# Attention feature sums moved from GpSimd to TensorE strips, with a later second decode and another streamed output weight pair

## The chip, the cores and the metric

One NeuronCore of a Trainium2 chip runs the whole program. The metric is the device time of one execution in microseconds (us), as the median of the runs shown.

## What is computed

A linear attention, and then a gated projection on its output:

```
proj = q @ w_phi;  proj -= max(|proj|) over the features;  phi = [exp(proj), exp(-proj)]   (the same for k)
kv  = sum over s of phi(k)[s, f] * v[s, d]
z   = sum over s of phi(k)[s, f]
att = (phi(q) @ kv) / (phi(q) @ z + 1e-6)
out = ((x @ w_a) * (x @ w_b)) @ w_out          with x = att, heads side by side
```

There are 8 batches of 8 heads, 576 positions, 64 channels a head and 128 features. x is 4608 x 512, w_a and w_b are 512 x 1536, and w_out is 1536 x 512. The three weights come as 64-bit floats and are turned into pairs of 32-bit floats (a high and a low part) on the core.

## The kernel before

The program has two stages, one after the other.

**Attention.** Two heads make a pair, and there are 32 pairs. `attention` (L259) walks i from 0 to 33. Of pair i it does the projections (`project_first`, `project_last`); of pair i-1 the product of features and values (`kv_products`); of pair i-2 the numerator and denominator (`num_products`, `den_products`), whose division (`reciprocals`) follows in steps placed by `turn`, four turns to a pair. TensorE takes its products strictly in the order in which they are written, since `pe` (L64) ties each to the one before. Three double banks of PSUM (`duo`, L263) go round among pq, pk, pn and pd.

The key features of a pair are `e` (128 positions by 2 heads by 4 chunks by 2 signs by 128 features), and `er` holds those of the last 64 positions of two pairs at once. For the queries the maximum runs over partitions, so GpSimd finds it with two all-reduces a pair (L169, tile mb), and VectorE subtracts it (L170). The feature sums z are made by `summed` (L175): GpSimd adds the four chunks to two (L180) and these to one (L182), VectorE adds the rest `er` (L185), and then `z_products` (L197) sums over the partitions by four products with a column block of ones, each for one 32-column strip of the array, into the third part of the PSUM tile kv. `kv_out` copies kv to the tile back, `turned_kv` transposes it (pt) and VectorE copies that to kvh, which the numerator and denominator need.

**Projection.** From L691 on, 12 blocks of 768 tokens follow: 6 with the first half of the hidden features (p = 0) and the same 6 with the second half (p = 1). `moe_block` (L522) uses seven products of half-size matrices in place of eight (`winograd`, L432, three quarters q a block), and each of these from three products of high and low parts. Their weights stand in DRAM (kept) and come back through a ring of four tiles (`refill`, L658): each time a product is done, `feed` (L700) fetches the next. Of w_out, ten pairs of factors stay on chip for all blocks of a half, and the last, a single one (`streamed`, L654), comes through the ring in each block.

**Decoding.** `load_factors` (L318) turns weights into factors: for each of two halves a load (raw, L327), one ScalarE and four VectorE operations, then seven sums and splits with a store each (L353). All of these transfers go through the queue of SyncE (SP). The first half's decoding is spread over the attention by `between` (L675). The second half's begins in block 0, a step at a time from `feed` (L710), at 1.2 steps a product; these steps are not held behind other work (`placed`, L638, holds those of the first half), so the scheduler may draw them forward.

Of the kernel before, what the change touches and what calls it, by code (L numbers as in the profile page):

```python
# [18 lines left out]
P = 128  # L19
# [4 lines left out]
LAG = 2  # L24
# [3 lines left out]
LAST_RATE = 1.2  # L28
# [7 lines left out]
def tile_kernel(ctx, tc, qP, km, kr, vm, vr, w_phi, eye, w_a, w_b, w_out, out):  # L36
# [56 lines left out]
    marks, loads, feeds, st = [], [], [], {}  # L93

    def attention_consts(a1, duo):
# [31 lines left out]
    def features(u, y, n, a1, a2):  # L127
# [3 lines left out]
        d = a1.tile([P, 2, n, F], F32, tag=f"d{n}", name=f"d_{u}")  # L131
# [25 lines left out]
    def project_last(i, a1, a2, consts, duo):  # L157
# [16 lines left out]

    def summed(i, a1, a2):  # L175

        e, er = st["e", i], st["er", i]
        two = a1.tile([P, 2, 2, 2 * F], F32, tag="two", name=f"two_{i}")
        ev = e.rearrange("p j c s f -> p j c (s f)")
        nc.gpsimd.tensor_tensor(two, ev[:, :, 0:2], ev[:, :, 2:4], op=ALU.add)  # L180
        z = st["z", i] = a2.tile([P, 2, 2 * F], F32, tag="z", name=f"z_{i}")
        nc.gpsimd.tensor_tensor(z, two[:, :, 0], two[:, :, 1], op=ALU.add)  # L182
        rows = heads[i % 2]
        rv = er.rearrange("p j c s f -> p j (c s f)")
        nc.vector.tensor_tensor(z[rows], z[rows], rv[rows], op=ALU.add)  # L185
# [11 lines left out]
    def z_products(i, consts):  # L197
        for n, (j, s) in enumerate(itertools.product(range(2), range(2))):
            mm(st["kv", i][strips[n], 2], consts[2], st["z", i][:, j, s * F : (s + 1) * F])

    def kv_out(i, a2):
        back = st["back", i] = a2.tile([P, 3, P], F32, tag="back", bufs=1, name=f"back_{i}")
        nc.scalar.copy(back, st["kv", i])
# [19 lines left out]
    def den_products(i, a2, duo):  # L223
# [7 lines left out]
        dn = a2.tile([P, HALF], F32, tag="dn", bufs=1, name=f"dn_{i}")  # L231
# [27 lines left out]
    def attention(a1, a2, ps, between):  # L259
# [17 lines left out]
        for i in range(NP + LAG):  # L277
# [4 lines left out]
            if num:  # L282
                turned_kv(i - LAG, a2, consts, ps)
            if new:
                project_last(i, a1, a2, consts, duo)
                summed(i, a1, a2)
            if kv_:
                kv_products(i - 1, ps)
            if i + 2 < NP:
                load(i + 2, a1, a2)  # L290
            turn(4 * i + 1)
            if num:
                num_products(i - LAG, a2, duo)
                turn(4 * i + 2)
                den_products(i - LAG, a2, duo)
                steps = reciprocals(i - LAG, a1, a2)
                later.extend((4 * i + 2 + t, steps) for t in REC_TURNS)
            else:
                turn(4 * i + 2)
            if kv_:  # L300
                z_products(i - 1, consts)
                kv_out(i - 1, a2)
            turn(4 * i + 3)
# [5 lines left out]
    outs = [[(p, q, "o", k) for k in FACTORS for q in range(NQ)] for p in range(2)]  # L309
# [8 lines left out]
    def load_factors(p, q, nm):  # L318
# [5 lines left out]
        for i in range(2):  # L324
            f = 2 * (NQ * p + q) + i
            raw = coded.tile([P, DM, 2], U32, tag="raw", name=f"raw_{p}{q}{nm}{i}")
            nc.sync.dma_start(raw.rearrange("p n w -> p (n w)"), src[f * P : (f + 1) * P, :].bitcast(U32))  # L327
# [17 lines left out]
        def stored(*names):  # L345
            for k in names:
# [6 lines left out]
                nc.sync.dma_start(kept[key][:, place], t.bitcast(F32))  # L353
# [78 lines left out]
    def winograd(p, j, q, xs, hs, spaces, feed):  # L432
# [36 lines left out]
        def lo(k, src):  # L469
            nc.vector.tensor_tensor(hs[k][1], src, hs[k][0], op=ALU.subtract)  # L470
# [51 lines left out]
    def moe_block(p, j, xs, x_next, spaces, feed):  # L522
# [75 lines left out]
        product(1, "w12", 1, late_)  # L598
        next(quads[-1])
# [54 lines left out]
    streamed = len(outs[0]) // 2 - 1  # L654
    order = deque(key for p in range(2) for _ in range(NB) for key in [(p, *key) for key in order] + [("o", p, streamed)])
# [17 lines left out]
    early = placed(codes[0])  # L673
# [23 lines left out]
    for p in range(2):  # L697
        own = deque(pair for pair in pairs if pair[:2] == ("o", p) and pair[2] != streamed)

        def feed():  # L700
# [4 lines left out]
            if own:  # L705
# [3 lines left out]
            if p == 0:  # L709
# [54 lines left out]
```

## Time and profile before

| | us |
|---|---|
| Median of 3 runs (lowest to highest) | 1614.45 (1613.93 to 1622.92) |
| The profiled execution, as timed | 1618.62 |
| Its span, from first to last instruction | 1616.8 |
| TensorE busy with products | 1191.3 |
| VectorE busy | 948.6 |
| ScalarE busy | 636.4 |
| GpSimd busy | 258.2 |

The span is that of one execution. Busy time of one engine lies beside that of the others, so these shares do not add up; what counts in a stage is who waits there for whom. The mean granted TensorE clock of the span is 0.862, where 1 stands for 2.4 GHz and the lower of the two levels, 1.2 GHz, would be 0.5. The first projection product begins 752.4 us into the span, so the attention stage takes 752.4 us and the twelve blocks 864.4 us.

### The profile page before, as it was taken

How to read it: one execution, taken by the hardware profiler on the slowest of the kernel's cores; microseconds unless marked ns; L12 is line 12 of the kernel's file. 1: busy time of each engine (PE TensorE's matmuls, PEld its weight loads, DVE VectorE, ACT ScalarE, POOL GpSimd, SP SyncE). 2: the span in 40 equal slices, each digit the busy share in tenths (PEclk: the TensorE clock that was granted, in tenths of full speed). 3: DMA queues.
4: the chain of work that ended last, by engine and by line, in shares of the span. 5: the costliest groups of instructions: out<-in, count | busy, mean ns of one | idle time of the engine just before them, and what ended most of it. 6: DMA issues, size and time to landing. Idle time of an engine off the chain costs nothing.

```text
span 1616.8 us, 20946 instructions
## 1 busy us (share of the span) xinstructions
PE 1191.3 (74%) x7394; PEld 1021.5 (63%) x7394; DVE 948.6 (59%) x1804; ACT 636.4 (39%) x1239; POOL 258.2 (16%) x132
## 2 busy tenths in 40 slices
PE   2736373564536355537798898999999999999998
PEld 2413241332313233325798888999999999999998
DVE  2354353354425346455687886758566686866865
ACT  3324242333324234333354444435344353443532
POOL 2333333334323333341000000000000000000000
PEclk7768687677767677767898999999999999999999
DMA  3225343332323343336988695766789677786774
GB/s 122 80 82 167 113 155 95 94 109 89 114 88 117 106 126 98 112 107 203 377 256 316 226 323 176 241 195 234 238 268 306 186 262 240 233 285 198 258 229 143
DMA packets 135673, 297.67 MB, mean 184 GB/s; under 512 B 22800, under 2 KB 53904, under 8 KB 135568
## 3 DMA queue, kind: packets, MB, share of 16 engines
q1 hardware_dynamic: 135264, 296.20, 55.5%
q8 instruction: 59, 0.97, 0.2%
q14 instruction: 46, 0.38, 0.1%
q10 hardware_dynamic: 304, 0.13, 0.0%
HBM read 234.64 MB, written 61.64 MB: 183 GB/s over the span
## 4 chain that ended last, share of the span: by engine, by line
PE 36%; DMA 10%; DVE 8%; issue 2%; ACT 1%; POOL 0%; SPq 0%; DVEq 0%; ACTq 0%; POOLq 0%
PE pa L430 12%; PE po L430 12%; PE pb L430 12%; DMA back_s<-kept_s 3%; DMA xx<-xnorm 2%; DMA back_w<-kept_w 1%; DVE hl_s L470 1%; DVE top L463 1%; DMA rb<-rec 1%; DMA rec<-r 0%; DVE hl_w L470 0%; DMA xnorm<-x 0%; DMA kept_o<-t_10o_s 0%; DMA raw_11o<-in_w_out 0%; DVE low L510 0%
## 5 line engine op out<-in xcount | busy, mean ns | idle before, releaser
L170 DVE TENSOR_TENSOR p<-p,mb 128x576 f32<-128x576 f32 x64 | 78.5, 1227 | 196.2 <-POOL mb L169 196.2
L78 PE MATMUL kv<-z,ones 128*32 128x128 f32 x256 | 18.6, 373 | 220.8 <-DVE z L185 220.8
L169 POOL PARTITION_ALL_REDUCE mb<-p x64 | 139.4, 2216 | 215.3 <-issue 91.3
L430 PE MATMUL po<-hh_s,back_o 128*128 128x384 f32 x576 | 163.1, 337 | 6.7 <-ACT hh_s L467 6.1
L78 PEld LDWEIGHTS kv<-z,ones 128*32 128x32 f32 x256 | 8.2, 136 | 235.7 <-DVE z L185 231.0
L78 PE MATMUL pn<-eq,kvh 128*64 128x288 f32 x512 | 93.1, 520 | 85.8 <-DVE kvh L211 84.1
L185 DVE TENSOR_TENSOR z<-z,e_r 64x512 f32<-64x512 f32 x32 | 22.0, 686 | 185.1 <-POOL z L182 185.1
L78 PEld LDWEIGHTS pn<-eq,kvh 128*64 128x64 f32 x512 | 47.9, 172 | 124.0 <-issue 93.6
L430 PE MATMUL po<-hh_w,back_o 128*128 128x384 f32 x432 | 119.0, 336 | 2.2 <-ACT o L547 1.6
L430 PEld LDWEIGHTS po<-hh_s,back_o 128*128 128x128 f32 x576 | 105.8, 189 | 9.2 <-ACT hh_s L467 7.4
L180 POOL TENSOR_TENSOR two<-e 128x1024 f32<-128x1024 f32 x32 | 78.2, 2443 | 199.5 <-issue 140.8
L430 PE MATMUL po<-hl_s,back_o 128*128 128x384 f32 x288 | 97.7, 339 | 3.4 <-DVE hl_s L470 3.2
L430 PEld LDWEIGHTS po<-hh_w,back_o 128*128 128x128 f32 x432 | 79.1, 189 | 3.0 <-ACT o L547 1.9
L539 DVE TENSOR_TENSOR o<-po,o 128x384 f32<-128x384 f32 x84 | 46.3, 556 | 56.1 <-PE po L430 42.3
L78 PE MATMUL pq<-q,w 64*128 64x288 f32 x256 | 69.8, 629 | 8.1 <-issue 7.0
L78 PE MATMUL pd<-eq,kvh 128*32 128x288 f32 x512 | 46.5, 490 | 35.9 <-DVE d L134 35.9
L430 PE MATMUL po<-hl_w,back_o 128*128 128x384 f32 x216 | 72.4, 335 | 0.0
L136 ACT ACTIVATE e<-d 128x1024 f32<-128x1024 f32 x32 | 33.8, 1057 | 93.8 <-DVE d L134 93.7
L78 PEld LDWEIGHTS pk<-w,k 64*128 64x128 f32 x512 | 54.1, 292 | 25.0 <-ACT x L221 19.7
L171 ACT ACTIVATE eq<-p 128x1152 f32<-128x1152 f32 x32 | 37.2, 1161 | 80.1 <-DVE p L170 80.1
L78 PE MATMUL kv<-e,v 128*64 128x256 f32 x512 | 67.6, 409 | 1.0 <-ACT e L137 1.0
L78 PE MATMUL pk<-w,k 64*128 64x128 f32 x512 | 55.7, 383 | 13.1 <-ACT x L221 13.1
(320 smaller groups left out, 3349.9 us busy)
## 6 DMA issues: line engine op xcount, KB each, us to landing
back_s<-kept_s SPq DMA_DIRECT2D x144, 512.0 KB
back_w<-kept_w SPq DMA_DIRECT2D x108, 512.0 KB
back_o<-kept_o SPq DMA_DIRECT2D x30, 512.0 KB
q<-in_qP SPq DMA_DIRECT2D x32, 288.0 KB
rb<-rec SPq DMA_DIRECT2D x64, 144.0 KB
xnorm<-x SPq DMA_DIRECT2D x32, 288.0 KB
xx<-xnorm SPq DMA_DIRECT2D x16, 576.0 KB
part<-o SPq DMA_DIRECT2D x48, 192.0 KB
```

The costliest lines, as they stand in the source:

```text
L78: return pe(lambda: nc.tensor.matmul(out, w, x, start=start, stop=stop, skip_group_check=True))
L136: nc.scalar.activation(e[:, :, :, 0], d, AF.Exp)
L169: nc.gpsimd.partition_all_reduce(mb, p32[:, j], P, bass_isa.ReduceOp.absmax)
L170: nc.vector.tensor_tensor(p32[:, j], p32[:, j], mb, op=ALU.subtract)
L171: nc.scalar.activation(eq[:, :, 0], p32, AF.Exp)
L180: nc.gpsimd.tensor_tensor(two, ev[:, :, 0:2], ev[:, :, 2:4], op=ALU.add)
L185: nc.vector.tensor_tensor(z[rows], z[rows], rv[rows], op=ALU.add)
L430: issued[0] = nc.tensor.matmul(*args, skip_group_check=True, **kwargs)
L463: nc.vector.tensor_tensor(to[:, i], acc[k][i], to[:, i], op=ALU.add)
L470: nc.vector.tensor_tensor(hs[k][1], src, hs[k][0], op=ALU.subtract)
L539: nc.vector.tensor_tensor(given[key], x, given[key], op=ALU.add)
```

## The change

1. **Feature sums.** `summed` is gone, and with it the two GpSimd sums and the VectorE sum of each pair. `z_products` now runs over the features themselves: 16 products of `e` (4 chunks by 2 heads by 2 signs) and 4 of `er`, each with a 32-column block of ones into one strip. For `er` the ones are zero in the half of the rows that belongs to the other pair.
2. **Order in the attention.** The products of z follow at once on those of kv, and `turned_kv` now follows in the same pass, between numerator and denominator of the pair before. The steps of the division begin one turn later. Tiles d, back and dn have two buffers.
3. **Second decoding.** Its steps begin in block 1, at 1.45 a product, each held behind the latest marked VectorE operation (also those of `lo` in `winograd` are marked now), and its loads and stores are issued by GpSimd, after the last all-reduce.
4. **w_out.** The streamed entry is now a pair, the two factors w11 and w12 of the last quarter, which is used early in the last part of a block; right after its last use (`spent`) the ring is refilled, where before that came at the block's end. The pairs that stay on chip are fetched at two of three products.

The diff, cut to its core:

```diff
-LAST_RATE = 1.2
+LAST_FROM, LAST_RATE = 1, 1.45
...
-        ones = a1.tile([P, D // 2], F32, name="ones")
+        ones = a1.tile([P, 3, D // 2], F32, name="ones")
         nc.vector.memset(ones, 1.0)
+        nc.vector.memset(ones[D:, 1], 0.0)
+        nc.vector.memset(ones[:D, 2], 0.0)
...
-            nc.gpsimd.partition_all_reduce(mb, p32[:, j], P, bass_isa.ReduceOp.absmax)
+            maxima.append(nc.gpsimd.partition_all_reduce(mb, p32[:, j], P, bass_isa.ReduceOp.absmax))
...
-    def summed(i, a1, a2):
-        e, er = st["e", i], st["er", i]
-        two = a1.tile([P, 2, 2, 2 * F], F32, tag="two", name=f"two_{i}")
-        ev = e.rearrange("p j c s f -> p j c (s f)")
-        nc.gpsimd.tensor_tensor(two, ev[:, :, 0:2], ev[:, :, 2:4], op=ALU.add)
-        z = st["z", i] = a2.tile([P, 2, 2 * F], F32, tag="z", name=f"z_{i}")
-        nc.gpsimd.tensor_tensor(z, two[:, :, 0], two[:, :, 1], op=ALU.add)
...
     def z_products(i, consts):
-        for n, (j, s) in enumerate(itertools.product(range(2), range(2))):
-            mm(st["kv", i][strips[n], 2], consts[2], st["z", i][:, j, s * F : (s + 1) * F])
+        ones, kv = consts[2], st["kv", i]
+        js = list(enumerate(itertools.product(range(2), range(2))))
+        for c in range(NFULL):
+            for n, (j, s) in js:
+                mm(kv[strips[n], 2], ones[:, 0], st["e", i][:, j, c, s], start=(c == 0), stop=False)
+        for n, (j, s) in js:
+            mm(kv[strips[n], 2], ones[:, 1 + i % 2], st["er", i][:, j, 0, s], start=False)
...
             turn(4 * i)
-            if num:
-                turned_kv(i - LAG, a2, consts, ps)
             if new:
                 project_last(i, a1, a2, consts, duo)
-                summed(i, a1, a2)
-            if kv_:
-                kv_products(i - 1, ps)
             if i + 2 < NP:
                 load(i + 2, a1, a2)
             turn(4 * i + 1)
+            if kv_:
+                kv_products(i - 1, ps)
+                z_products(i - 1, consts)
+                kv_out(i - 1, a2)
+            turn(4 * i + 2)
             if num:
                 num_products(i - LAG, a2, duo)
+            if kv_:
+                turned_kv(i - 1, a2, consts, ps)
+            turn(4 * i + 3)
+            if num:
                 den_products(i - LAG, a2, duo)
...
+            queue = nc.gpsimd if p else nc.sync
+            behind(maxima if p else [], lambda: queue.dma_start(raw.rearrange("p n w -> p (n w)"), rows))
...
-                nc.sync.dma_start(kept[key][:, place], t.bitcast(F32))
+                queue.dma_start(kept[key][:, place], t.bitcast(F32))
...
         product(1, "w12", 1, late_)
+        spent()
...
-    streamed = len(outs[0]) // 2 - 1
+    order = deque(key for p in range(2) for _ in range(NB) for key in [(p, *key) for key in order] + [("o", p, 0)])
...
-            if own:
+            if own and used[0] % 3:
...
-            if p == 0:
-                steps(codes[1], 0, LAST_RATE)
+            if p == 0 and j >= LAST_FROM:
+                steps(late, 0, LAST_RATE)
```

On GpSimd the program before alternates between two kinds of work in each pair. These rows of its order are from the third and fourth pair; a bare `ISA` without operands stands at each change of kind, `ISA` with mb is an all-reduce, and two and z are the sums.

```order
L180 TENSOR_TENSOR two_312<-e_279 128x1024
L169 ISA
L169 ISA mb_0_304<-p_2_261 128x576
L169 ISA mb_1_307<-p_2_261 128x576
L182 ISA
L182 TENSOR_TENSOR z_314<-two_312 128x512
L169 ISA
L169 ISA mb_0_419<-p_3_372 128x576
L169 ISA mb_1_422<-p_3_372 128x576
L180 ISA
L180 TENSOR_TENSOR two_427<-e_390 128x1024
```

The same two pairs and the next one on GpSimd in the changed program:

```order
L171 ISA mb_0_312<-p_2_275 128x576
L171 ISA mb_1_315<-p_2_275 128x576
L171 ISA mb_0_438<-p_3_395 128x576
L171 ISA mb_1_441<-p_3_395 128x576
L171 ISA mb_0_584<-p_4_531 128x576
L171 ISA mb_1_587<-p_4_531 128x576
```

The sums are gone and the all-reduces follow on each other. Before, there are 72 bare `ISA` rows on GpSimd; now there are 3, one of them ahead of the first all-reduce.

On TensorE, one pass before, from the sixth pair's projections on (the x behind a row counts products; a product of 32-bit floats takes two instructions):

```order
L78 MATMUL pq_0_632<-q_5_445,w_100 128x288 x2
L78 MATMUL pk_636<-w_100,k_5_443 128x128 x8
L209 MATMUL pt_653<-ident,back_623 128x128 x3
L78 MATMUL pq_1_659<-q_5_445,w_100 128x288 x2
L78 MATMUL kv_677<-e_518,v_4_336 64x256 x8
L78 MATMUL kv_677<-e_r_550,rv_334 64x256 x2
L78 MATMUL pn_701<-eq_418,kvh_657 64x288 x8
L78 MATMUL pd_715<-eq_418,kvh_657 32x288 x8
L78 MATMUL kv_677<-z_564,ones 32x128 x4
```

And one pass of the changed program, of the same pair:

```order
L78 MATMUL pq_0_674<-q_5_448,w_100 128x288 x2
L78 MATMUL pk_678<-w_100,k_5_446 128x128 x8
L78 MATMUL pq_1_700<-q_5_448,w_100 128x288 x2
L78 MATMUL kv_723<-e_549,v_4_328 64x256 x8
L78 MATMUL kv_723<-e_r_580,rv_326 64x256 x2
L78 MATMUL kv_723<-e_549,ones 32x128 x16
L78 MATMUL kv_723<-e_r_580,ones 32x128 x4
L78 MATMUL pn_760<-eq_437,kvh_656 64x288 x8
L204 MATMUL pt_771<-ident,back_754 128x128 x3
L78 MATMUL pd_780<-eq_437,kvh_656 32x288 x8
```

The four products on z have become twenty on e and er, ahead of pn and no longer last in the pass, and pt has gone from the pass's first half to a place between pn and pd.

On SP, the queue before has the second decoding's transfers (raw, and kept from t, of the weights 10a and 10b) among those of the attention's divisions (xnorm, rec, rb):

```order
L327 DMA raw_10b_4473<-in_w_b 128x1024
L353 DMA kept_0_w_4360<-t_10a_w_4357 128x512
L353 DMA kept_0_s_4382<-t_10a_s_4379 128x512
L256 DMA xnorm_79<-x_27_3722 128x576
L353 DMA kept_0_s_4443<-t_10a_s_4440 128x512
L247 DMA rec_72<-r_3880 128x9
L353 DMA kept_0_s_4449<-t_10a_s_4446 128x512
L251 DMA rb_3972<-rec_72 64x576 x2
```

In the changed program these transfers stand on GpSimd, behind the last all-reduce (of pair 31):

```order
L171 ISA mb_1_4244<-p_31_4210 128x576
L323 DMA raw_10a_5197<-in_w_a 128x1024
L323 DMA raw_10a_5252<-in_w_a 128x1024
L349 DMA kept_0_w_5345<-t_10a_w_5342 128x512
L349 DMA kept_0_w_5350<-t_10a_w_5347 128x512
L323 DMA raw_10b_5482<-in_w_b 128x1024
```

All 81 of them, 18 loads and 63 stores, have left SP. Of the second decoding's VectorE rows, 51 stand in the attention before, 25 in block 0, 51 in block 1 and 39 in block 2; now 4 stand in block 0 and 31, 36, 36, 32 and 28 in blocks 1 to 5.

## Rows read from the trace of the kernel before

**Rows 1.** Groups of instructions on GpSimd: count, then busy us, mean ns, idle before.

```profile
L169 POOL PARTITION_ALL_REDUCE mb<-p x64 | 139.4, 2216 | 215.3 <-issue 91.3 <-PE pq L78 18.1 <-PE pk L78 17.5
L180 POOL TENSOR_TENSOR two<-e 128x1024 f32<-128x1024 f32 x32 | 78.2, 2443 | 199.5 <-issue 140.8 <-DVE r L245 15.7 <-DVE w_01b L339 8.0
L182 POOL TENSOR_TENSOR z<-two 128x512 f32<-128x512 f32 x32 | 40.4, 1262 | 66.6 <-issue 57.6 <-ACT t_00a_w L87 7.2
```

**Rows 2.** Timeline of GpSimd: start us, us, instruction, idle before it.

```profile
343.80 2.33 POOL L180 TENSOR_TENSOR two<-e 128x1024 f32<-128x1024 f32 x1 [8.40 <-issue]
...
353.37 4.30 POOL L169 PARTITION_ALL_REDUCE mb<-p  x2 [5.91 <-issue]
364.90 2.33 POOL L180 TENSOR_TENSOR two<-e 128x1024 f32<-128x1024 f32 x1 [7.23 <-issue]
373.14 4.30 POOL L169 PARTITION_ALL_REDUCE mb<-p  x2 [5.91 <-issue]
```

**Rows 3.** Timeline of ScalarE, the inputs of the two at 343.80 and 353.37.

```profile
340.12 0.62 ACT L163 COPY p<-pq 128x576 f32<-128x576 f32 x1
...
341.60 1.04 ACT L137 ACTIVATE e<-d 128x1024 f32<-128x1024 f32 x1
```

**Rows 4.** Stretches: us, busy (instructions) of PE, PEld, DVE, ACT, POOL; clock, DMA.

```profile
0.00:752.00 752.00, 379.08 (x2858) 223.82 (x2858) 336.61 (x548) 270.34 (x434) 258.16 (x132) 0.73 0.35 111
...
387.00:398.00 11.00, 10.85 (x87) 6.73 (x91) 6.42 (x13) 4.41 (x6) 4.72 (x3) 0.74 0.38 122
398.00:407.00 9.00, 8.97 (x95) 5.51 (x87) 5.97 (x6) 6.33 (x9) 3.20 (x2) 1.00 0.44 142
```

**Rows 5.** Timeline of TensorE, two passes in a row.

```profile
387.15 0.65 PE L78 MATMUL kv<-z,ones 128*32 128x128 f32 x8 [23.30 <-DVE z L185]
...
398.05 0.40 PE L78 MATMUL kv<-z,ones 128*32 128x128 f32 x8
...
405.83 1.18 PE L78 MATMUL pd<-eq,kvh 128*32 128x288 f32 x16
```

**Rows 6.** Timeline of the SP queue (transfers issued), one pass.

```profile
396.60 0.38 SPq L247 DMA_DIRECT2D rec<-r  x1
400.05 1.11 SPq L251 DMA_DIRECT2D rb<-rec  x2
401.26 0.52 SPq L234 DMA_DIRECT2D den<-dn  x1
403.41 0.32 SPq L242 DMA_DIRECT2D r<-den  x1
...
406.25 0.38 SPq L121 DMA_DIRECT2D rv<-in_vr  x1
```

**Rows 7.** Timeline of VectorE, behind an all-reduce.

```profile
399.09 1.88 DVE L170 TENSOR_TENSOR p<-p,mb 128x576 f32<-128x576 f32 x1 [2.05 <-POOL mb L169]
```

**Rows 8.** Timeline of TensorE, the attention's opening and end.

```profile
14.68 0.60 PE L78 MATMUL kv<-e_r,rv 128*64 128x256 f32 x4
...
752.41 0.45 PE L430 MATMUL pa<-xw11h,back_w 128*128 128x384 f32 x1 [0.81 <-ACT dn L232]
```

**Rows 9.** Stretches as in rows 4: blocks 0, 1, 2 and 3.

```profile
752.00:821.00 69.00, 55.59 (x292) 53.79 (x293) 47.49 (x103) 28.45 (x67) 0.00 (x0) 0.93 0.89 327
821.00:905.00 84.00, 73.46 (x382) 71.09 (x380) 67.03 (x147) 39.56 (x91) 0.00 (x0) 0.92 0.82 277
905.00:988.00 83.00, 73.19 (x384) 70.77 (x385) 66.19 (x145) 38.99 (x91) 0.00 (x0) 0.94 0.78 266
988.00:1055.00 67.00, 65.36 (x376) 64.89 (x376) 44.85 (x91) 29.31 (x63) 0.00 (x0) 1.00 0.67 218
```

**Rows 10.** Waits of TensorE, 850 to 1010: us in total, times, longest.

```profile
PE pa L430 <- DMA back_s<-kept_s: 7.6, 3, 3.5
...
PE pa L430 <- DMA back_w<-kept_w: 2.6, 2, 1.8
```

**Rows 11.** Waits of TensorE, 1010 to the end.

```profile
PE pa L430 <- DMA back_s<-kept_s: 9.1, 8, 1.6
```

More of the change, by code (lines that the diff above doesn't have):

```diff
@@ L92, in tile_kernel @@
     times = [slice(t * HALF, (t + 1) * HALF) for t in range(2)]
-    marks, loads, feeds, st = [], [], [], {}
+    marks, loads, feeds, maxima, st = [], [], [], [], {}
     def attention_consts(a1, duo):
@@ L291, in attention @@
             turn(4 * i + 1)
+            if kv_:
[3 more added lines that the diff above has]
+            turn(4 * i + 2)
             if num:
                 num_products(i - LAG, a2, duo)
-                turn(4 * i + 2)
+            if kv_:
+                turned_kv(i - 1, a2, consts, ps)
+            turn(4 * i + 3)
+            if num:
                 den_products(i - LAG, a2, duo)
                 steps = reciprocals(i - LAG, a1, a2)
[L297 to L303, printed above, removed]
+                later.extend((4 * i + 3 + t, steps) for t in REC_TURNS)
         for t in range(4 * (NP + LAG), 4 * (NP + LAG) + 10):
@@ L308, in tile_kernel @@
     pairs = {(p, q, k): [(p, q, nm, k) for nm in "ab"] for p in range(2) for q in range(NQ) for k in FACTORS}
-    outs = [[(p, q, "o", k) for k in FACTORS for q in range(NQ)] for p in range(2)]
+    late_o = [(NQ - 1, k) for k in FACTORS[:2]]
+    late_o += [(q, k) for k in FACTORS for q in range(NQ) if (q, k) not in late_o]
+    outs = [[(p, q, "o", k) for q, k in late_o] for p in range(2)]
     for p in range(2):
@@ L326, in load_factors @@
             raw = coded.tile([P, DM, 2], U32, tag="raw", name=f"raw_{p}{q}{nm}{i}")
-            nc.sync.dma_start(raw.rearrange("p n w -> p (n w)"), src[f * P : (f + 1) * P, :].bitcast(U32))
+            queue = nc.gpsimd if p else nc.sync
+            rows = src[f * P : (f + 1) * P, :].bitcast(U32)
+            behind(maxima if p else [], lambda: queue.dma_start(raw.rearrange("p n w -> p (n w)"), rows))
             yield
@@ L671, in steps @@
             next(gen, None)
-    early = placed(codes[0])
+    early, late = (placed(code) for code in codes)
     def between(t):
@@ L697, in tile_kernel @@
     for p in range(2):
-        own = deque(pair for pair in pairs if pair[:2] == ("o", p) and pair[2] != streamed)
+        own = deque(pair for pair in pairs if pair[:2] == ("o", p) and pair[2])
         def feed():
@@ L714, in tile_kernel @@
             x_next = factors_of_x(*divmod(n_, NB), xs) if n_ < 2 * NB else iter(())
-            moe_block(p, j, xs, x_next, spaces, feed)
-            if order:
-                refill()
+            moe_block(p, j, xs, x_next, spaces, feed, lambda: refill() if order else None)
         if p == 0:
-            for _ in codes[1]:
+            for _ in late:
                 pass
```

14 lines of the change are left out of this document (5 added, 9 removed).

## The prediction

> **What bounds the kernel now.** The windows come first. The attention takes 752 us, and no engine is busy for more than half of it: 379 us of products, 337 of VectorE, 270 of ScalarE, 258 of GpSimd [rows 4]. So something waits in turn, and the groups by line say what. GpSimd's three groups are busy for 139.4 + 78.2 + 40.4 = 258.0 us and idle before them for 215.3 + 199.5 + 66.6 = 481.4 us [rows 1]. Together that is 739.4 us: GpSimd is either working or idle ahead of its own next instruction from the stage's first microsecond to its end. By its share it looks like the least loaded engine, and yet the stage lasts as long as its chain.
>
> The question is whether that idle time is a wait for data. The timeline of GpSimd shows a gap of 5.91 us ahead of an all-reduce each time one follows a sum, and of 7.23 to 8.40 us ahead of a sum that follows an all-reduce [rows 2]. The all-reduce at 353.37 reads query projections that ScalarE finished at 340.12 + 0.62 = 340.74, almost 13 us earlier [rows 3]; nothing it needs was late. And the program's order has a bare row at each such change of kind, 72 before and 3 now. I read the gap as GpSimd's own price of changing between all-reduce and sum, about 481.4 / 70 = 6.9 us each. A pair then costs GpSimd 139.4/32 + 78.2/32 + 40.4/32 = 8.1 us of work and up to 5.9 + 7.2 us of change, 21.2 us; the stage has 752.4/32 = 23.5 us a pair.
>
> The chain from there to TensorE is short: the products on z wait for the sum, kv, back, pt and kvh follow, and TensorE takes its products in order, so the whole next pass stands behind it (23.30 us of idle time ahead of one such product [rows 5]). The twelve blocks after 752.41 [rows 8] are another matter: there products run nearly without a gap, 65.36 of 67 us at a granted clock of 1.00 in block 3 [rows 9].
>
> **The change, part by part.** *The sums.* GpSimd loses 118.6 us of work and nearly all changes of kind; what stays is 139.4/32 = 4.4 us a pair. VectorE loses the sum of z. TensorE has twenty products a pair for four. Four took 0.40 us at the full clock and 0.65 us at a lower one [rows 5], so twenty take at most five times that, and the addition is at most 1.6 us (2.6 us at the lower). At least nothing is gained there: the columns stream through either way. I take the upper end, as the row is of the same shape.
>
> *What is late next.* The pass from 398.05 to the end of pd at 405.83 + 1.18 = 407.01 had no sum ahead of it: 8.96 us, at a clock of 1.00 (2.4 GHz), after TensorE had been busy for 10.85 of 11 us. The pass before it took 398.05 - 387.15 = 10.90 us at a mean clock of 0.74, after 23 us of idleness [rows 4, 5]. With z that is 8.96 + 1.6 = 10.6 us and 10.90 + 2.6 = 13.5 us. If the clock stayed at the lower level (0.5, 1.2 GHz) a line through these two passes against 1/clock gives 14.3 + 2.6 = 16.9 us, an estimate. The other engines ask for less or about as much: VectorE 337/32 = 10.5 us with the sum and the part of the second decoding that leaves the stage, so near 9; ScalarE 8.4; GpSimd 4.4. SP issues a pass's transfers and waits twice in it for a transfer to land: from 396.60 to 406.63 in one pass, 3.07 of it ahead of rb and 1.63 ahead of r [rows 6], so 10.0 us, and with xnorm and two or three stores of the first decoding (0.4 each) about 11.4 us. VectorE subtracts the maxima only when the all-reduce is through, and the first subtraction beside the second all-reduce lasted 1.88 us after a wait of 2.05 [rows 7]; as nothing in this loop (4.4 us of all-reduce, two subtractions, two exponentials) exceeds 9 us, it is a source of small waits and no bound.
>
> So a pass lies between 10.6 us (TensorE full, everything else beneath it) and 16.9 us. Several loops of 9 to 11.4 us meet in engines that work in order, so I don't take the lowest; the nearest row is the pass at clock 0.74, and I take 13.0 us.
>
> *The stage.* The opening reaches the end of the first kv products at 14.68 + 0.60 = 15.3 us without any sum [rows 8]. Then come 30 full passes, and I allow 15 us for the last two short ones (about 8 us of products, then a copy, pn and pd). 15.3 + 30 x 13.0 + 15 = 420 us in place of 752.4: a gain of 332 us. With 10.6 us it is 348, with 16.9 us 537.
>
> A rule speaks against part of this. The tiling page of the Trainium skill (TensorEngine Tiling (Array Packing), Tiling Modes) says that changing the tiling mode drains TensorE. The new pass alternates between 64-, 32- and 128-column blocks once more than the old. No row prices a drain by itself, and by the rule the passes would be somewhat longer than the sum; the allowance from 10.6 to 13.0 us is worked out without it.
>
> *Second decoding and ring.* Block 3, without decoding, takes 67 us; blocks 0 to 2 take 69, 84 and 83, 35 us more, for 47.49 + 67.03 + 66.19 - 3 x 44.85 = 46.2 us more of VectorE work [rows 9]. That is 0.76 us of time a us of decoding, for 25 + 51 + 39 = 115 VectorE rows, 0.40 us each. Now 163 of these rows lie in blocks 1 to 5, 65 us of work: at the same price 50 us, a loss of 15. What the new queue may take away is this: of TensorE's idle time in 850 to 1010, 10.2 us were waits for ring weights [rows 10], whose transfers stood on SP behind the stores and loads of the decoding, and the stage has 160 - 2 x 67 = 26 us over in about that stretch. If that part goes, the price falls by some 40%, to 30 us: a gain of 5. Between -5 and +15 I take +2. The ring is refilled earlier in each block; the waits that it could spare are 9.1 us in the later blocks [rows 11], of which I take half, -5. The block stage moves by -3 us, between -15 and +15.
>
> A second rule bears on the queue. The DMA page of the Trainium skill (DMA: Bandwidth & Descriptors, Issuing engines are not separate DMA queues) says that transfers issued from several engines run on the same DMA engines and that only issue time is saved. If that held for the ring's waits, the decoding would keep its old price and the stage would lose 10 us in place of gaining 3. No run here shows it yet.
>
> *What hides the 81 transfers on GpSimd.* GpSimd has no other work in the blocks. No row shows a transfer issued there; between SP's 0.32 us [rows 6] and a whole change of kind, 7.2 us, I take the length of a sum, 2.3 us: 186 us within the 340 us of blocks 1 to 5, so nothing. At 7.2 us it would be 583 us and the second half's weights would be 243 us late.
>
> **The sum.** 1616.8 - 332 - 3 = 1282 us of span; the profiled execution was timed at 1618.62, 1.8 above its span, and the median of the runs lies 4.2 below that: 1282 + 1.8 - 4.2 = 1279.6, say 1280 us. A measurement of this kernel tells changes of about 1% from none.
>
> **The rivals.** *TensorE alone sets the pass.* With 10.6 us a pass the time is 1280 - 72 = 1208 us. For it: the second free pass took 8.96 us with everything in place. Against it: that was one pass, with work stored up by a long wait. 0.17.
>
> *The clock stays low and the in-order queues trip each other.* The mean clock of the stage was 0.73 [rows 4]; passes with short gaps might not raise it. With 16.5 us a pass: 1280 + 105 = 1385 us. Against it: the clock rose within one full pass. 0.18.
>
> *The new queue is slow.* If each transfer on GpSimd costs a change of kind, second-half weights are 243 us late: 1523 us. It decides from about 340/81 = 4.2 us a transfer on. Nothing speaks for it but the gaps of rows 2. 0.05.
>
> *The gaps were waits for data, and the time rises.* The sum at 343.80 began only 1.16 us after its exponentials ended at 342.64 [rows 2, 3]; if that were the rule and the all-reduces too waited for their inputs, taking the sums away would shorten nothing, and the longer products of z, on the same chain, would add 32 x 1.6 to 2.6 us: with +15 for the blocks about 1614 + 67 + 15 = 1696 us. It decides if GpSimd never had its data more than a us or so before it began. The all-reduce at 353.37 speaks against it. 0.03.
>
> That the change does not do what it says (the changes of kind persist in another form, and the time stays within 1%) gets 0.02.
>
> **How the numbers follow.** My own case, passes of 12 to 14.5 us, has 0.55 and spans 1250 to 1325 us. The range for 8 in 10 takes in most of the two neighbours: 1215 to 1390. Faster by over 1%: 0.55 + 0.17 + 0.18 + 0.05 = 0.95; within 1%: 0.02; slower by over 1%: 0.03.
>
> **What would show it.** In the changed profile GpSimd should have the all-reduces alone, without gaps of 6 us that nothing explains, and the windows should show a stage of some 420 us with TensorE busy for three quarters of it or more at a clock above 0.73. Waits for z vanish; those of SP for rec and den, of pd for d and of VectorE for mb should head the list. Blocks 1 to 5 should be alike, near 70 us, and block 0 near 67. I am wrong if passes still take 20 us, if an engine other than GpSimd shows gaps of several us at each pass, or if block 6 waits for its weights.

## The result and the profile after

The changed kernel takes 1320.43 us (median of 4 runs, 1316.53 to 1323.94) beside 1615.78 us for the kernel before: a ratio of 0.8165, with an interval from 0.8126 to 0.8204. The profiled execution was timed at 1316.53 us and spans 1314.4 us. Three stretches say where the time went; the columns are those of [rows 4], and the stretches are the attention, the first six blocks and the last six. After:

```profile
0.00:419.40 419.40, 336.12 (x3882) 206.60 (x3882) 301.32 (x479) 259.01 (x417) 142.94 (x69) 0.93 0.59 186
419.40:886.00 466.60, 416.13 (x2268) 401.88 (x2269) 339.21 (x722) 206.71 (x464) 44.15 (x80) 0.97 0.77 264
886.00:1314.40 428.40, 404.02 (x2270) 396.98 (x2268) 289.20 (x573) 167.16 (x358) 0.00 (x0) 0.99 0.69 225
```

The two stretches of blocks in the kernel before:

```profile
752.40:1207.00 454.60, 415.07 (x2268) 405.24 (x2269) 325.65 (x683) 200.19 (x447) 0.00 (x0) 0.96 0.76 259
1207.00:1616.80 409.80, 397.11 (x2270) 392.49 (x2268) 286.38 (x573) 165.47 (x358) 0.00 (x0) 1.00 0.71 236
```

The attention went from 752.4 to 419.4 us. The blocks went the other way, from 864.4 to 895.0 us: 12.0 us more in the first half and 18.6 in the second. So two questions were left for the runs: whether the attention fell for the reason given, and what in the rest of the change costs the blocks 31 us. In the attention TensorE's busy time fell from 379.08 [rows 4] to 336.12 us although it has 1024 more instructions, at a mean granted clock of 0.93 after 0.73.

Of the three groups of [rows 1] one is left on GpSimd, and what it waits for now has a name, ScalarE's copies of p. The gaps of 5.9 and 7.2 us of [rows 2] are gone. The GpSimd group by line, then its timeline (start, duration, instruction, idle time before):

```profile
L171 POOL PARTITION_ALL_REDUCE mb<-p x64 | 142.2, 2264 | 258.8 <-ACT p L165 222.7 <-DVE p L172 12.8 <-DVE r L240 10.9
```

```profile
216.94 4.59 POOL L171 PARTITION_ALL_REDUCE mb<-p  x2 [10.90 <-DVE r L240]
225.36 4.30 POOL L171 PARTITION_ALL_REDUCE mb<-p  x2 [3.83 <-ACT p L165]
240.88 4.52 POOL L171 PARTITION_ALL_REDUCE mb<-p  x2 [11.22 <-ACT p L165]
```

TensorE's timeline shows a pass that waits for nothing, the counterpart of [rows 5]. Where before only four z products stood, there are sixteen on e and four on e_r (the page counts two records for each):

```profile
220.76 0.76 PE L78 MATMUL pq<-q,w 64*128 64x288 f32 x4
...
225.35 1.08 PE L78 MATMUL kv<-e,ones 128*32 128x128 f32 x32
226.25 0.40 PE L78 MATMUL kv<-e_r,ones 128*32 128x128 f32 x8
226.58 2.16 PE L78 MATMUL pn<-eq,kvh 128*64 128x288 f32 x16
...
230.40 0.76 PE L78 MATMUL pq<-q,w 64*128 64x288 f32 x4
```

This pass takes 230.40 - 220.76 = 9.64 us; the twenty products take 226.58 - 225.35 = 1.23 us of it, to the start of the next group. Passes with waits are longer. TensorE's waits in the attention, then SP's (total us, times, longest):

```profile
PE pt L204 <- ACT back L198: 29.5, 20, 3.6
PE pk L78 <- ACT x L216: 29.3, 15, 5.2
PE pq L78 <- ACT dn L227: 12.7, 9, 3.1
```

```profile
SPq L246 <- DMA rec<-r: 54.5, 24, 6.5
SPq L237 <- DMA den<-dn: 38.6, 28, 2.4
```

All three of TensorE's are copies by ScalarE, an engine that is busy for only 259 of 419 us. Its timeline, and then the product that waits, show why a copy is late although the engine has time over:

```profile
233.98 0.65 ACT L328 ACTIVATE raw_02b<-raw_02b 128x512 f32<-128x512 f32 x1 [5.22 <-DMA raw_02b<-in_w_b]
234.53 0.62 ACT L216 COPY x<-pn 128x576 f32<-128x576 f32 x1
```

```profile
235.21 2.08 PE L78 MATMUL pk<-w,k 64*128 64x128 f32 x16 [4.06 <-ACT x L216]
```

Ahead of the copy of x stands a step of the first decoding, which waits 5.22 us for its weights. Such waits of ScalarE for the decoding's loads (raw) and stores (kept) add up to 88 us in the attention, and most of TensorE's longer waits for x and dn follow one. No run moves these steps, so what they cost is not shown.

### The profile page after: what moved, and what is told of

It is laid out like the page before. It is cut to its first block, busy times and chain, and to the rows that moved or that the text cites. A ratio compares the mean times of both kernels' runs of the same rounds, so it can differ in the third digit from the quotient of the medians.

```text
span 1314.4 us, 22642 instructions
## 1 busy us (share of the span) xinstructions
PE 1156.3 (88%) x8418; PEld 1005.5 (76%) x8418; DVE 929.7 (71%) x1774; ACT 632.9 (48%) x1239; POOL 187.1 (14%) x149
## 5 line engine op out<-in xcount | busy, mean ns | idle before, releaser
L463 ACT CAST hh_s<-top 128x384 fp32r<-128x384 f32 x72 | 36.9, 514 | 78.1 <-DVE top L502 72.2
L78 PE MATMUL pn<-eq,kvh 128*64 128x288 f32 x512 | 69.4, 414 | 0.0
L78 PE MATMUL pq<-q,w 64*128 64x288 f32 x256 | 52.5, 489 | 16.4 <-ACT dn L227 12.7
L426 PE MATMUL pa<-xs1h,back_s 128*128 128x384 f32 x144 | 45.0, 350 | 17.0 <-DMA back_s<-kept_s 14.7
L78 PEld LDWEIGHTS kv<-e,v 128*64 128x64 f32 x512 | 37.2, 151 | 28.9 <-issue 12.7
L459 DVE TENSOR_TENSOR top<-pa,top 128x384 f32<-128x384 f32 x72 | 39.8, 553 | 27.5 <-PE pa L426 25.2
L426 PEld LDWEIGHTS po<-hl_s,back_o 128*128 128x128 f32 x288 | 54.8, 190 | 2.9 <-DVE hl_s L466 2.9
L426 PE MATMUL pa<-xs3h,back_s 128*128 128x384 f32 x144 | 45.5, 357 | 12.0 <-ACT top L455 10.3
L249 DVE TENSOR_TENSOR x<-x,rb 128x576 f32<-128x576 f32 x32 | 33.5, 1048 | 31.3 <-DMA rb<-rec 26.8
L172 DVE TENSOR_TENSOR p<-p,mb 128x576 f32<-128x576 f32 x64 | 53.2, 831 | 2.1 <-POOL mb L171 2.0
L78 PEld LDWEIGHTS pn<-eq,kvh 128*64 128x64 f32 x512 | 34.0, 137 | 26.2 <-issue 6.1
```

The source lines that it names most:

```text
L78: return pe(lambda: nc.tensor.matmul(out, w, x, start=start, stop=stop, skip_group_check=True))
L249: behind(marks, lambda: nc.vector.tensor_tensor(x32, x32, rb, op=ALU.mult))
L426: issued[0] = nc.tensor.matmul(*args, skip_group_check=True, **kwargs)
L459: nc.vector.tensor_tensor(to[:, i], acc[k][i], to[:, i], op=ALU.add)
L463: nc.scalar.copy(hs[k][0], src)
```

## The experiments

Each run stands beside runs of the kernel before on the same chip (medians 1615 to 1618 us). "Stages" are the attention, first half and second half of its one profiled execution. Executions of one kernel lie up to 16 us apart (sums_alone 1289.16 to 1305.46), so a difference of a few us in one stage of two profiles says little.

**Does GpSimd pay for the change of kind?** `kind_change` puts one tiny sum a pair back:

```diff
         st["eq", i] = eq
+        tiny = a2.tile([P, 8], F32, tag="tiny", name=f"tiny_{i}")
+        nc.gpsimd.tensor_tensor(tiny, mb[:, :8], mb[:, 8:16], op=ALU.add)
```

> The changed kernel with one tiny sum a pair put back on GpSimd (128 x 8 elements, on a tile that nothing reads), so that all-reduces and sums alternate again. Theory (GpSimd pays about 5.9 us for a change to an all-reduce and 7.2 us for one to a sum, whatever the sum's size): a pass then takes at least 4.4 + 5.9 + 7.2 = 17.5 us for the 13.0 us now, the attention 419 + 32 x 4.5 = 563 us, the total about 1460 us, with the two gaps a pair back in GpSimd's timeline. Rival (the sums' own length and their data were the cost): a sum of 8 elements takes well under 1 us, so about 1322 us and no gaps.

Measured: 1496.93 us, ratio 0.9268 [0.9228, 0.9308]; attention 597.9 us, blocks 895.4. GpSimd's timeline and groups:

```profile
262.24 0.19 POOL L177 TENSOR_TENSOR tiny<-mb 128x8 f32<-128x8 f32 x1 [7.36 <-DVE w_02a L337]
268.75 4.30 POOL L171 PARTITION_ALL_REDUCE mb<-p  x2 [6.32 <-issue]
280.21 0.19 POOL L177 TENSOR_TENSOR tiny<-mb 128x8 f32<-128x8 f32 x1 [7.16 <-DVE w_02a L337]
```

```profile
L171 POOL PARTITION_ALL_REDUCE mb<-p x64 | 137.6, 2190 | 216.9 <-issue 168.7 <-ACT p L152 31.1 <-ACT p L165 8.8
L177 POOL TENSOR_TENSOR tiny<-mb 128x8 f32<-128x8 f32 x32 | 8.5, 266 | 232.9 <-issue 52.8 <-DVE r L242 42.2 <-DVE r L241 22.4
```

Both gaps are back around a sum that lasts 0.19 us, and the pass is 280.21 - 262.24 = 17.97 us. The sum reads what the all-reduce just before it wrote, so the engine named as releaser is a guess of the page. The idle time is (216.9 + 232.9) / 64 = 7.0 us a change, as in the kernel before (6.9). The sum brings back 597.9 - 419.4 = 178.5 of the 333 us that the attention had lost. The rest lies mostly in the sums themselves: before, GpSimd had 258.0 us of work and 481.4 of idle time [rows 1], here it has 146.1 and 449.8, which is 112 us less of work and 32 less of idle time. The theory's 1460 us was made of the smaller gaps of [rows 2] and comes out 37 low. Blocks of 895 us show that nothing else moved. The rival is out by 175 us. The second buffers of d, back and dn stand in every run, so what they add was not tried apart.

**Does the new order of the pass matter?** `old_order` is the changed kernel with the pass in its old order:

```diff
+            if num:
+                turned_kv(i - LAG, a2, consts, ps)
             if new:
                 project_last(i, a1, a2, consts, duo)
+            if kv_:
+                kv_products(i - 1, ps)
...
+            if num:
+                num_products(i - LAG, a2, duo)
+                turn(4 * i + 2)
+                den_products(i - LAG, a2, duo)
...
             if kv_:
-                kv_products(i - 1, ps)
                 z_products(i - 1, consts)
                 kv_out(i - 1, a2)
-            turn(4 * i + 2)
-            if num:
-                num_products(i - LAG, a2, duo)
-            if kv_:
-                turned_kv(i - 1, a2, consts, ps)
```

> The changed kernel with the attention's pass in the order of the kernel before (turned back first, kv behind the key projection, z on the strips behind den, division steps one turn earlier). Theory (the sums on GpSimd were nearly the whole cost, the order only small waits): attention 420 to 450 us, total 1315 to 1345 us. Rival (the new order carries a large part, because z and back come at the pass's end and the next pass stands behind them): attention above 500 us, total above 1400 us.

Measured: 1304.65 us, 0.8075 [0.8048, 0.8103]; stages 417.8, 462.5, 424.3. The attention is as long as with the new order (419.4), so the order carries none of the gain. The total is even below that of the changed kernel; see `sums_old`, and what stays open.

**What do the w_out and decode edits do?** Five kernels take them back singly and together.

`w_out_back` undoes the three w_out edits:

```diff
-    late_o = [(NQ - 1, k) for k in FACTORS[:2]]
...
+    outs = [[(p, q, "o", k) for k in FACTORS for q in range(NQ)] for p in range(2)]
...
-        spent()
...
-            if own and used[0] % 3:
+            if own:
...
+            if order:
+                refill()
```

> The changed kernel with its w_out edits undone: the single last factor is streamed, the ring is refilled for it at the block's end, and the resident pairs are fetched at every product. Theory (the streamed pair and the refills around it cost the blocks): the second half, which has no decoding, returns from 428 to about 410 us and TensorE's waits for back_o (13 us) go; about 1320 - 18 - 10 = 1292 us. Rival (the order that the scheduler finds for the second half is chance, or the waits for back_o are only where a wait for another ring entry would stand): 1315 to 1325 us with the second half still near 425. If the edits gain, as my prediction had it by 5 us: 1325 or more.

Measured: 1307.18 us, 0.8081 [0.8053, 0.8109]; stages 423.8, 469.6, 412.2. Of the 31 us the second half's 16 go, the first half's part stays: the total lies between the two expectations. The theory holds for the second half (412.2). In the first the rival's second case holds: TensorE's waits for back_o (12.0 us) are gone, but those for back_s went from 20.9 to 30.4 us.

`same_queue` changes one line of the changed kernel:

```diff
-            queue = nc.gpsimd if p else nc.sync
+            queue = nc.sync
```

> The changed kernel with the second decoding's loads and stores issued by SP again, all else as changed. Theory (SP's queue held up the ring behind the decoding's transfers, so the new queue gains some 20 us of decoding price): 1335 to 1345 us, with more waits of TensorE for back_s and back_w in blocks 1 to 5. Rival (transfers share the same DMA engines, the queue makes no difference): 1315 to 1325 us.

Measured: 1317.54 us, 0.8166 [0.8142, 0.8191]; stages 422.5, 457.1, 427.8. No difference in the total, so the theory that I held, a queue that spares the ring its waits, falls. The profiled execution is the shortest of its four (1309.21 us, the others 1316.75 to 1324.04), so its first half of 457.1 us is no sure sign of a gain; `late_sp` tests this once more.

`decode_back` puts the second decoding back whole (start, rate, placing and queue), with the w_out edits kept:

```diff
-LAST_FROM, LAST_RATE = 1, 1.45
+LAST_FROM, LAST_RATE = 0, 1.2
...
-    early, late = (placed(code) for code in codes)
+    early, late = placed(codes[0]), codes[1]
```

> The changed kernel with the second decoding as before: from block 0, 1.2 steps a product, not held back, on SP. Part of it then lies in the attention again, which no longer waits for GpSimd. Theory (decoding costs about 0.76 us a us of VectorE work wherever it falls, and in a full attention it is no longer free): 1320 to 1340 us, with the attention longer than 419 us. Rival (the late and spread decoding is what costs the first half its 12 us): 1300 to 1310 us.

Measured: 1312.68 us, 0.8128 [0.8095, 0.8161]; stages 429.0, 450.8, 426.7. The first half gets 15.8 us shorter, the attention, which takes some decoding back, 9.6 longer. The total lies between the two expectations: the attention is longer, as the theory had it, and the first half gives its 12 us and more, as the rival had it. The interval overlaps that of the changed kernel, so a gain in the total by this edit alone is not shown.

`sums_alone` has both edits of the two above.

> The changed kernel with both the w_out edits and the decoding edits undone: only the feature sums and the new order of the attention stay. Theory (the sums make the whole gain, the other parts lose some 20 us together): 1290 to 1305 us, attention 420 to 430 us, second half 410 us. Rival (the other parts gain as a whole): 1330 us or more.

Measured: 1294.00 us, 0.8018 [0.7977, 0.8058]; stages 423.5, 451.7, 412.2. This is the theory's number: the feature sums and the pass's order make the gain, and the rest of the change gives 26 us of it back. How the 26 divide depends on the order: taken back first, the w_out edits give 13 (1320.4 - 1307.2) and the decode edits then 13 (1307.2 - 1294.0); the other way round it is 8 for decoding (1320.4 - 1312.7) and 19 for w_out.

`late_sp` is w_out_back with the decoding's transfers on SP (the one line of same_queue):

> The kernel of w_out_back (w_out edits undone; 1307 us, first half 470 us) with the second decoding's transfers back on SP; the decoding still begins a block later, placed, at 1.45 steps a call. It tells the queue from the lateness in the first half's 18 us over sums_alone (452 us, 1294 us). Theory (the lateness costs: 27 more VectorE rows in the blocks by 0.4 us and a first half that is decoded up to its last block; the queue nothing): first half 465 to 470 us, total 1303 to 1309 us. Rival (transfers issued on GpSimd hold up the ring's: TensorE's ring waits were 34.5 us in w_out_back's first half and 41.7 in the changed kernel's, against 27.8 with same_queue): first half 457 to 460 us, total 1294 to 1299 us.

Measured: 1304.88 us, 0.8077 [0.8040, 0.8113]; stages 424.2, 465.3, 413.0. Beside w_out_back the queue changes nothing: the totals lie 2.3 us apart, inside their intervals, and TensorE's ring waits (back_s and back_w) in the first half are 34.4 us here and 34.5 there. What is left beside sums_alone is the lateness, which means the later start, the higher rate and the placing together; these were not tried apart. The two totals do not carry this alone, since their intervals overlap, but apart from decode_early, further below, the profiles fall in two groups: the first half takes 450.8 to 454.6 us in the six kernels that decode as before and 457.1 to 469.6 us in the six that decode late. TensorE's block 5 (the last of the first half) in `late_sp`, and in `sums_alone`, as windows:

```profile
792.50:889.50 97.00, 86.87 (x457) 83.31 (x456) 67.87 (x146) 40.95 (x92) 0.00 (x0) 0.93 0.79 259
```

```profile
791.80:875.20 83.40, 80.49 (x458) 78.87 (x457) 53.95 (x109) 33.99 (x74) 0.00 (x0) 1.00 0.77 245
```

With 13.92 us more of VectorE work block 5 lasts 13.6 us longer; all of the first half's 13.6 us (465.3 - 451.7) stands in this block, what blocks 0 to 2 gain and blocks 3 and 4 lose being about even. TensorE's waits in the block, in `late_sp` and in `sums_alone`:

```profile
PE pa L424 <- DMA back_s<-kept_s: 5.0, 2, 4.1
PE po L424 <- ACT hh_s L461: 4.1, 2, 2.8
```

```profile
PE pa L424 <- DMA back_s<-kept_s: 1.5, 1, 1.5
PE po L424 <- ACT hh_s L461: 1.2, 1, 1.2
```

With the smaller ones the waits grew by 7.0 us; 6.4 us more (86.87 - 80.49) are TensorE's busy time, at a granted clock of 0.93 against 1.00; what lowered the clock is not shown. The first half as a whole has only 7.9 us more of VectorE work (339.30 against 331.42), so a price for each us of that work does not describe its 13.6 us. And the attention, from which the decoding's first rows have gone (24 on VectorE in sums_alone, by their start times), is no shorter (424.2 against 423.5).

**Which w_out edit costs the second half its 16 us?** `pair_only` is sums_alone with the streamed pair alone, `pair_spent` has the early refill too.

```diff
-    outs = [[(p, q, "o", k) for k in FACTORS for q in range(NQ)] for p in range(2)]
+    late_o = [(NQ - 1, k) for k in FACTORS[:2]]
+    late_o += [(q, k) for k in FACTORS for q in range(NQ) if (q, k) not in late_o]
+    outs = [[(p, q, "o", k) for q, k in late_o] for p in range(2)]
...
-    streamed = len(outs[0]) // 2 - 1
-    order = deque(key for p in range(2) for _ in range(NB) for key in [(p, *key) for key in order] + [("o", p, streamed)])
+    order = deque(key for p in range(2) for _ in range(NB) for key in [(p, *key) for key in order] + [("o", p, 0)])
...
-        own = deque(pair for pair in pairs if pair[:2] == ("o", p) and pair[2] != streamed)
+        own = deque(pair for pair in pairs if pair[:2] == ("o", p) and pair[2])
```

> The kernel of sums_alone (feature sums on the strips, second decoding and w_out as before: 1294 us, second half 412 us) with one of the three w_out edits, the other streamed pair; the ring is refilled at a block's end as before and every call may fetch a kept pair. Theory (which pair is streamed decides the order in which TensorE takes the products at a block's end, the order of the kernel after, and this order is what costs): second half about 428 us, total about 1310 us. Rival (the early refill is what costs, by its transfers): second half 412 us, total 1294 us.

> pair_only with the early refill as well (two of the three w_out edits; TensorE's order is that of pair_only). Theory (the order costs, the early refill changes nothing that TensorE waits for): the same as pair_only within 6 us, 1305 to 1315 us. Rival (the early refill costs): pair_only at 1294 and this one at 1310 us. Third way (the early refill was meant to pay for the pair and does): pair_only well above this one, 1320 us against 1305.

Measured: pair_only 1316.72 us, 0.8149 [0.8115, 0.8183], stages 429.3, 453.6, 432.0; pair_spent 1319.24 us, 0.8172 [0.8146, 0.8199], stages 430.2, 453.4, 434.6. Both are as the theories had it in kind, with totals 7 and 4 us above what they expected. So the pair alone costs the second half 432.0 - 412.2 = 19.8 us, and the early refill changes nothing clear of noise. All thirteen profiles agree: the second half takes 409.8 to 413.3 us in the six kernels that stream the single factor and 424.3 to 434.6 in the seven that stream the pair, whatever came before. The third w_out edit, fetching at two of three products, is what separates decode_back from pair_spent: 1312.7 against 1319.2 us, with intervals that overlap. TensorE's order where block 3 of the second half begins (tile x products; the numbers behind pa and pb are half, block and group, each counted from 0, and po belongs to the block that ends) in sums_alone, then in pair_only:

```
pa_1_2_2x6 pb_1_2_2x6 pa_1_3_0x6 pb_1_3_0x6 po_1_2_0x7 po_1_2_1x7
po_1_2_0x6 po_1_2_1x4 pb_1_2_2x6 po_1_2_1x2 pa_1_3_0x6 po_1_2_0x6 pb_1_3_0x6 po_1_2_1x5
```

TensorE's waits in the second half, in sums_alone and in pair_only:

```profile
PE pa L424 <- ACT top L453: 4.6, 5, 1.7
PE pa L424 <- DMA back_s<-kept_s: 3.2, 4, 1.4
...
PE pa L424 <- DMA back_w<-kept_w: 0.6, 1, 0.6
```

```profile
PE pa L426 <- ACT top L455: 10.9, 6, 3.2
PE pa L426 <- DMA back_w<-kept_w: 4.3, 4, 1.6
PE pa L426 <- ACT low L455: 2.9, 2, 2.3
PE po L426 <- DMA back_o<-kept_o: 2.0, 3, 1.5
```

Other products now stand between pa and pb of the next block's first product, and what grew most is the wait for ScalarE to empty the banks, top and low: 6.3 + 2.9 us. The waits for weights grew by 3.7 + 2.0 - 1.8, and TensorE's busy time by 7.3 (405.59 against 398.26 us, at a clock of 0.98 against 1.00). That makes 20.4 us of 19.8. That the pair costs is shown; that it does so by the order more than by its transfers is read from these rows and was not tried apart.

**A better version?** `sums_old` is sums_alone with the old order of the pass, so only the feature sums and their buffers are left of the change. `decode_early` is sums_alone with the second decoding strung behind the first in the attention:

```diff
-DECODE_FROM, DECODE_RATE = 3, 1.22
+DECODE_FROM, DECODE_RATE = 3, 2.44
...
-    early, late = placed(codes[0]), codes[1]
+    early, late = placed(itertools.chain(*codes)), iter(())
```

> The kernel of sums_alone with the attention's pass in the order of the kernel before: of the whole change only the feature sums on the strips are left (with the buffers that go with them), all else is the kernel before. Theory (the sums are the whole gain, the pass's order is neutral as in old_order): attention 418 to 428 us, first half 452, second 412, total 1280 to 1300 us. Rival (the new order is worth something once the w_out and decode edits are gone): above 1305 us.

> The kernel of sums_alone with the second decoding strung behind the first in the attention, twice as many decoding steps a turn: 135 of its VectorE rows stand in the attention (27 in sums_alone) and 36 in the first half's blocks (144). Theory (in the attention, where VectorE is busy for 300 of 420 us, decoding lies beside other work, while in the blocks each us of it costs about 0.76 us): the first half loses 108 x 0.40 x 0.76 = 33 us, 452 to about 419 us, the attention grows by at most 10, total 1261 to 1275 us. Rival (VectorE's queue is in the attention's loop as much as in the blocks): the attention grows by the 43 us of added work or more, total 1290 to 1310 us.

Measured: sums_old 1286.05 us, 0.7944 [0.7900, 0.7988], stages 420.5, 452.1, 413.3, as its theory expected and the best of all, though its interval meets that of sums_alone; decode_early 1320.28 us, 0.8156 [0.8122, 0.8190], stages 477.6, 425.5, 411.6. The rival holds for decode_early, with a total 10 us above its range: beside sums_alone 26.2 us come off the first half and 54.1 are added to the attention. Its stretch of attention and its largest wait of TensorE:

```profile
0.00:477.60 477.60, 357.35 (x3882) 216.07 (x3882) 359.08 (x610) 284.52 (x478) 147.93 (x68) 0.87 0.63 204
```

```profile
PE pt L204 <- ACT back L198: 93.4, 28, 7.3
```

VectorE did 42.7 us more work (359.08 against 316.42 in sums_alone), ScalarE 21.4, and TensorE's wait for back went from 31 to 93 us. VectorE has a quarter of the stage free in both kernels, and still the stage grew by more than VectorE's added work. Whether VectorE's added work does this or ScalarE's, which makes the copy back, was not tried apart.

## Why the prediction was right, and where it was off

The total, 1280 us, was 40 below the measured 1320, inside the range; in the profiled execution 1314.4 us of span stand for the 1282 summed up. Nearly all of the difference lies in the blocks.

- *GpSimd's gaps are a price of changing kind.* Shown by kind_change: 7.0 us a change round a sum of 8 elements a partition, against the 6.9 that the prediction took from [rows 1]. The first step of that argument proves nothing, though: work and idle time add up to the stage's length on every engine, so 739.4 of 752 us does not make GpSimd the limit. What carries it is that most of the idle time has no named releaser ("issue") and that the input was ready almost 13 us before [rows 3]. The Trainium skill (GPSIMD Engine Reference, Instruction dispatch) says that the first call to a freshly loaded kernel on GpSimd costs about 6 us more, with no instruction in the profile. The 5.91 to 6.32 us in the rows shown ahead of an all-reduce agree with it, the 7.16 to 8.40 us ahead of a sum are longer; that the gaps are such loads is the account of the Trainium skill, no run here shows the loading itself.
- *The attention's 420 us.* Measured 419.4. The mean pass by the same allowances is (419.4 - 30.3) / 30 = 12.97 us for the 13.0 taken. But the mix is another one. The prediction took 13.0 from a pass without waits at a clock of 0.74. The free pass took 9.64 us for the 10.6 summed up, mostly since the twenty z products took 1.23 us where the prediction allowed 2.0 (0.40 and 1.6 more); the mean clock of the stage was 0.93; and 83.3 of the 419.4 us (419.4 - 336.1), 2.6 us a pair, are idle time of TensorE. So the close hit is luck in part: two errors of opposite sign, a pass priced too long and waits left out.
- *What is late next.* Waits for z are gone, SP's waits for rec and den head its list as foreseen [rows 6], and TensorE was busy for 336 of 419 us, over three quarters. VectorE's wait for mb came to 2.0 us in all and pd's for d does not show. What holds up TensorE instead is ScalarE, by back, x and dn, 71.5 us; the prediction had priced ScalarE by its sum, 8.4 us a pass, and not by what stands in its order ahead of the copies, such as the first decoding's steps with their waits for transfers.
- *The drain between tiling modes.* In the free pass the 32-column products on e_r end, by the modelled end, at 226.65 and the 64-column pn starts at 226.58. The Trainium skill (TensorEngine Tiling (Array Packing), Tiling Modes) has a change of mode drain TensorE; this trace shows no time for it, as far as modelled ends can tell.
- *"The block stage moves by -3 us, between -15 and +15."* This is the step that failed: it moved by +30.6. It had two terms. The decoding, +2, measured +12.0 (466.6 - 454.6): the old price alone, +15, was nearly right, and of the relief by the new queue that was set against it same_queue and late_sp show nothing. The old price was near in size only, since late_sp finds most of the cost in one block and not spread with the work. By start times in the traces the second decoding has 30, 55 and 49 VectorE rows in blocks 0 to 2 before (37 in the attention) and all 171 in blocks 1 to 5 after, where the prediction counted 115 and 163. TensorE's waits for ring weights in the first half grew (first before, then after); those for back_o come with the new streamed pair, as w_out_back has none:

```profile
PE pa L430 <- DMA back_s<-kept_s: 13.2, 8, 3.5
PE pa L430 <- DMA back_w<-kept_w: 12.5, 5, 7.7
```

```profile
PE pa L426 <- DMA back_s<-kept_s: 20.9, 14, 6.8
PE po L426 <- DMA back_o<-kept_o: 12.0, 5, 5.4
PE pa L426 <- DMA back_w<-kept_w: 8.8, 7, 2.0
```

  The Trainium skill (DMA: Bandwidth & Descriptors, Issuing engines are not separate DMA queues) has transfers from all engines run on the same DMA engines. Same_queue and late_sp agree: 1317.5 against 1320.4 us, 1304.9 against 1307.2. The ring, -5, measured +18.6 (428.4 - 409.8). In the second half the waits for ring weights did not even shrink (first before, then after):

```profile
PE pa L430 <- DMA back_s<-kept_s: 4.6, 5, 1.4
```

```profile
PE pa L426 <- DMA back_w<-kept_w: 4.8, 6, 1.5
PE po L426 <- DMA back_o<-kept_o: 1.3, 2, 0.8
PE pa L426 <- DMA back_s<-kept_s: 0.5, 1, 0.5
```

  Those for back_s went from 4.6 to 0.5 us, as hoped, but back_w and back_o came up: 6.6 us in all for 4.6. And the prediction took the streamed pair for a change of transfers only, while it also changes TensorE's order; the pair costs 19.8 us by pair_only.
- *Transfers on GpSimd.* Taken at 2.3 us each, hidden; 80 of the 81 lie in the blocks and keep GpSimd busy for 44 us there, about 0.55 us each, well under the 4.2 from which the slow-queue rival decides. Hidden they are.
- *Blocks 1 to 5 near 70 us, block 0 near 67.* They took 70.9 (block 0), 76.2, 74.9, 76.9, 76.8 and 90.9. Blocks 1 to 4 are even, as foreseen, but longer. Block 5 was taken for one like the others; it is a long one without decoding too (83.4 us in sums_alone, with 458 products where block 3 has 373).
- *The rivals.* A pass of 10.6 us throughout and one of 16.5 both miss the measured 12.97; the gaps as waits for data would have given 1696.

What stays open: why the kernels with the old order of the pass are some 8 to 16 us faster in total (old_order against the changed kernel, intervals apart; sums_old against sums_alone, intervals that touch), though their attention is shorter by under 4. And of the first half's 14 to 18 us for the late decoding, block 5 is shown, but not which part of the lateness does it, nor why work there costs its full length while decode_early puts the price of the blocks' decoding at 26.2 us for 41.8 us of VectorE work (331.42 - 289.61), 0.63. What in the streamed pair costs, the order or the transfers, stays open too.

## What to carry to other kernels

When an engine with a small busy share shows gaps of much the same length whenever its kind of instruction changes, test it with an instruction of almost no size: if the gaps stay, taking that kind off the engine is worth the gaps as well as the work. Here the gaps alone brought back 178 of 333 us. Take a bundle of edits apart stage by stage: here the feature sums alone gave 330 us (1615.8 - 1286.1, sums_old) and the rest of the change gave 34 of them back, most of it in the blocks. An edit that looks like a choice of transfers can change the program's order on another engine; compare the orders before pricing it.

## What the runs showed of the hardware

- GpSimd's price for alternating all-reduces and sums was the same for the three sizes of sum here: 7.0 us a change on the average round sums of 0.19 us, and 6.9 with sums of 1.3 and 2.4 us together. It falls in both directions: in the rows shown 6.32 us ahead of an all-reduce, 7.16 and 7.36 ahead of a sum.
- Transfers issued on GpSimd had no such price: about 0.55 us each, and median landing times of 2.3 to 7.8 us for the different tiles beside the ring's traffic.
- Twenty products of a 32-column block of ones with 128 feature columns took 1.23 us at a granted clock of 1.00, with no visible gap at either end.
